# Epsilon added to the query features on VectorE, and output blocks evicted in 576 columns, in a fused convolution and linear-attention kernel

## The chip, the cores and the metric

The kernel runs on one core of a Trainium2 chip. The metric is the device time of one execution in microseconds; each version is run several times, and the median counts. A profiled execution gives a trace besides: which engine worked when, and on what. The engines are TensorE (PE in the profile, with its weight loads as PEld), VectorE (DVE), ScalarE (ACT), GpSimd (POOL) and SyncE (SP), which here only issues transfers (DMAs).

## The reference, cut to what matters

Two independent halves stand side by side in the last axis of the output, 576 columns each, for 2048 rows.

```python
# half A: a short convolution of k (4 taps), times v, then a causal convolution as long as the sequence, times q
for t in range(ks):
    k_shift = k_shift + k_pad[:, t:t + S, :] * shift_k[:, ks - 1 - t][None, None, :]
kv = k_shift * v
y_f = rfft(kv_pad) * rfft(kf_pad)          # length 2 * S
y = irfft(y_f)[:S] + kv * ssm_D
a = q * y
# half B: linear attention, 32 heads of 18 columns
phi = lambda t: jnp.where(t > 0, t + 1, jnp.exp(t)) + 1e-6
pq, pk = phi(q), phi(k)
kv = einsum("bhsd,bhse->bhde", pk, v);  z = einsum("bhsd->bhd", pk)
num = einsum("bhqd,bhde->bhqe", pq, kv)
den = einsum("bhqd,bhd->bhq", pq, z)[..., None] + 1e-6
b = (num / den) @ wo
```

Inputs and output are bfloat16. The change concerns the 1e-6 in `pq`, and the way in which the rows of `b` leave the chip.

## The kernel before, in words

**Half B.** x lies in four tiles of 512 rows; its transposes xT come from TensorE and PSUM for the first (L323) and by transposing transfers for the others (L347). Sixteen blocks of keys (L623) and twenty of queries (L644) are projected; ScalarE takes exp (L628, L647) and VectorE forms phi without the epsilon: pk by rows, and pqT, transposed, as two tiles of 128 x 5 x 1024 (feature in the partition, 126 features in each of four chunks and 72 in the fifth). G = x transposed times phi(k) (L673) is folded with the value weights into kv (L708), which is masked into heads as kvb (L711, L715), and with wo into M (L770), one 576 x 576 matrix in five chunks. The denominators (L744 to L761) become reciprocals, rden, which are written to DRAM and read back as rb, spread over the 18 features of each head; pqT is multiplied by rb in place, chunk by chunk, by VectorE or GpSimd (named pqn in the program). An output block of 128 rows is then five matmuls of pqT by M for each half of 288 columns (L813), each half evicted from its own PSUM bank into ob by ScalarE or VectorE, and one transfer of 144 KB for a block.

**The epsilon before.** (pq + 1e-6) times M is pq times M plus 1e-6 times the column sums of M over each head. The fifth chunk has only 72 features, so partitions 96 to 127 of it are free: there lie the 32 heads' reciprocals in pqT (two transfers from DRAM, named rh, after a memset at L280) and 1e-6 times the 32 column sums in M (ten matmuls, L798, an eviction by VectorE, L801, after a memset at L790). So the fifth chunk is contracted over 128 partitions.

**Half A.** The taps are VectorE products (L402) and sums, partly on GpSimd and partly by an accumulating transfer. The sequence is then transformed in two stages: 128-point matmuls by the table Gsb (L467, results Ch and Cu), VectorE transposes of 32x32 (L506), 16-point matmuls (L515, results sph and spu); a pointwise complex product of both (two products of 2048 columns, one of them with a copy X of sph whose neighbouring partitions are exchanged; 18 transfers on SP); the inverse 16-point stage (L551, results V) and 128-point stage (L576) by the table Esb; and the product with q. For two of three column groups an inverse result is evicted as yb first, and two such are multiplied at once.

**What sets the order.** Every step is recorded as an operation, and its engine and its place in the order come from a string, PLAN (a letter for the engine and the operation's number); PLACES gives each tile's address. Each engine runs its own list in that order and waits at the head of it. GpSimd's products wait for VectorE's last product ahead of them in the plan, so that the two take turns. SP issues nearly all transfers, in its order. Helpers record many operations under one line: L222 transfers, L229 ScalarE copies, L231 VectorE copies, L236 products and sums.

Of the kernel before, what the change touches and what calls it, by code (L numbers as in the profile page):

```python
# [13 lines left out]
S = 2048  # L14
D = 576
# [9 lines left out]
HDT = []  # L25
ACC = [(0, 1), (2, 1)]
# [88 lines left out]
def _tables():  # L115
# [11 lines left out]
    E = np.empty((128, 32 + 2, 128), np.float32)  # L127
# [3 lines left out]
    W = np.zeros((32, 3, 32), np.float32)  # L131
    for bb in range(16):
        for k1 in range(16):
            p = 2.0 * np.pi * ((k1 * bb) % 16) / 16.0
            c, s = np.cos(p), np.sin(p)
            W[bb, 0, 2 * k1] = c
            W[16 + bb, 0, 2 * k1] = s
            W[bb, 0, 2 * k1 + 1] = -s
            W[16 + bb, 0, 2 * k1 + 1] = c
            W[2 * k1, 1, 2 * bb] = c  # L140
# [8 lines left out]
    for i in range(2):  # L149
        E[:, 32 + i, :] = np.kron(np.eye(4), W[:, 1 + i, :])  # L150

# [17 lines left out]
    C[:, o:o + 8] = EPS  # L169
# [14 lines left out]
def kernel(  # L184
# [24 lines left out]
    w_d = nc.dram_tensor("w_scr", (4, D), BF, kind="Internal").ap()  # L209
# [24 lines left out]

    def tt(e, o, a, b, op):
        return (nc.vector if e == "DVE" else nc.gpsimd).tensor_tensor(out=o, in0=a, in1=b, op=op)  # L236
# [10 lines left out]
    Esb = SB("Esb", [128, 34, 128], side=1)  # L247
    srow = SB("srow", [64, D // 64, 4])
    srt = SB("srt", [64, 4, D // 64])
    wtok = P.buf("wtok", [128, 1], space="dram")  # L250
# [28 lines left out]
    for f in range(2):  # L279
        P.op("G", lambda e, f=f: nc.gpsimd.memset(pqT[f].t[64:128, 4, :], 0.0), wr=[(pqT[f], (4, g)) for g in (2 * f, 2 * f + 1)] + [(pqT[f], "r")], name="pqz", ms=1024, st="pqz%d" % f)  # L280
# [5 lines left out]
    load("srow", srow, lambda e: dma(e, srow.t[:], A_shift_k.rearrange("(p d) j -> p d j", p=64)), 4608, 72, engs=EARLY)  # L286
    for i in range(2):
# [3 lines left out]
    load("Esb", Esb, lambda e: dma(e, Esb.t[:].rearrange("p a c -> p (a c)"), E_d), 1114112, 8704)  # L291

    P.op("AD", lambda e: copy(e, srt.t[:], srow.t[:].rearrange("p d j -> p j d")), rd=[srow], wr=[srt], name="wjt", n=36)
    load("ww", None, lambda e: dma(e, ap(w_d, 0, [[D // 64, 64], [D, 4], [1, D // 64]]), srt.t[:]), 4608, 18, rd=[srt], wr=[wtok])
    load("wjb", Wj, lambda e: dma(e, Wj.t[:].rearrange("p j d -> p (j d)"), ap(w_d, 0, [[0, 128], [1, 4 * D]])), 589824, 4608,
         rd=[wtok], wr=[(Wj, 0), (Wj, 1)])
# [94 lines left out]
    def conv_piece(cc, bh):  # L391
# [12 lines left out]
        P.op("D", tap, rd=[kh, (Wj, 0)] + ([(Wj, 1)] if cc else []), wr=[(m, 0), (m, 2)], name="tap",  # L404
# [81 lines left out]
    def s2(C, cc, pp, nm):  # L486
# [23 lines left out]
        for kh in range(4):  # L510
            ps = psb(1, "s2ps")

            def mm(e, kh=kh, ps=ps):
                for j in range(4):
                    nc.tensor.matmul(  # L515
                        ps.t[32 * j:32 * j + 32, 0, :],
                        lhsT=W2()[32 * kh:32 * kh + 32, :], rhs=ct.t[32 * kh:32 * kh + 32, 8 * j:8 * j + 8],
                        start=True, stop=True)
            P.op("P", mm, rd=[ct, idw], wr=[ps], name="s2" + nm, st=st, mm=[(512, 32, 32)] * 4)
            P.op("AD", lambda e, kh=kh, ps=ps: copy(  # L520
                e, view(sp.t[:], 32 * kh, [[256, 8], [128, 2], [1, 32]]), ps.t[:, 0, :].rearrange("p (w k t) -> p w t k", w=8, t=2)),
                 rd=[ps], wr=[(sp, kh)], name="s2ev" + nm, n=512, st=st)
# [9 lines left out]
    def inv(g, su):  # L532
# [5 lines left out]
        xb = SB("X", [128, 16, 128])  # L538
        for i in range(2):
            load("X", xb, lambda e, i=i: dma(e, xb.t[i:128:2], tx.t[1 - i:128:2]), 262144, 4096, rd=[tx], wr=[(xb, i)])  # L540
        P.op("DG", lambda e: tt(e, xb.t[:], su.t[:], xb.t[:], ALU.mult),
             rd=[su], wr=[xb], name="p2", n=2048, x2=1, two=1, st=st)
        P.op("DG", lambda e: tt(e, tx.t[:], su.t[:], tx.t[:], ALU.mult),
             rd=[su], wr=[tx], name="p1", n=2048, x2=1, two=1, st=st)
        for hh in range(4):
            ps = psb(1, "i1ps")

            def mm(e, hh=hh, ps=ps):
                for c in range(4):
                    for wi, src in ((0, tx), (1, xb)):  # L550
                        nc.tensor.matmul(ps.t[:, 0, 128 * c:128 * c + 128], lhsT=src.t[:, 4 * hh + c, :], rhs=Esb.t[:, 32 + wi, :],  # L551
                                         start=(wi == 0), stop=(wi == 1))
            P.op("P", mm, rd=[tx, xb, Esb], wr=[ps], name="i1", st=st, mm=[(128, 128, 128)] * 8)

            def ev(e, hh=hh, ps=ps):
                copy(e, view(V[gi].t[:], c0 + 4 * hh, [[n, 32], [CC // 4, 4], [1, 4]]),
                     ps.t.rearrange("p b c -> p (b c)").rearrange("p (c j r) -> p r j c", j=4, r=32))
            P.op("AD", ev, rd=[ps], wr=[(V[gi], (g, hh))], name="i1ev", n=512, st=st)
# [4 lines left out]
    def inv2(gi):  # L563
# [5 lines left out]
        for bg in range(16 // nb):  # L569
# [10 lines left out]
            if gi in YA:  # L580
# [23 lines left out]
            ns = max(nb, 4)  # L604
# [30 lines left out]
    def qproj(c, g):  # L635
        h0, hn = HCH[c]
        ps = psb(1, "qps")
        eb = SB("eq", [128, 512])
# [3 lines left out]
        def mm(e):  # L642
            for t in range(5):
                nc.tensor.matmul(ps.t[0:hn, 0, :], lhsT=wq.t[0:KT[t], t, h0:h0 + hn], rhs=xT.t[0:KT[t], t, :],  # L644
                                 start=(t == 0), stop=(t == 4))
        P.op("P", mm, rd=[xT, wq], wr=[ps], name="q", mm=[(512, 128, 126)] * 5, st=st)
        P.op("A", lambda e: nc.scalar.activation(  # L647
            out=eb.t[0:hn], in_=ps.t[0:hn, 0, :], func=ACTF.Exp, bias=neg1.t[0:hn, :]), rd=[ps, neg1], wr=[eb],
             name="qexp", n=512, st=st)
        P.op("D", lambda e: nc.vector.scalar_tensor_tensor(  # L650
            out=pqT[g // 2].t[0:hn, c, 512 * (g % 2):512 * (g % 2) + 512], in0=eb.t[0:hn],
            scalar=1.0, in1=ps.t[0:hn, 0, :], op0=ALU.min, op1=ALU.max), rd=[ps, eb], wr=[(pqT[g // 2], (c, g))], name="qphi",
             n=512, st=st)
# [3 lines left out]
    for g in range(4):  # L657
        for c in range(5):
            qproj(c, g)
# [116 lines left out]
    for f in range(2):  # L776
# [3 lines left out]
        for c, (h0, hn) in enumerate(HCH):  # L780
            rb = SB("rb", [128, 1024])
# [3 lines left out]
            P.op("DG", lambda e, c=c, hn=hn, rb=rb, f=f: tt(e, pqT[f].t[0:hn, c, :], pqT[f].t[0:hn, c, :],  # L785
                                                           rb.t[0:hn, :], ALU.mult),
                 rd=[rb], wr=[(pqT[f], (c, g)) for g in (2 * f, 2 * f + 1)], name="pqn", n=1024, x2=1, two=1)
        load("rh", None, lambda e, f=f: dma(e, pqT[f].t[96:128, 4, :], ap(r_d, 1024 * f, [[2 * S, 32], [1, 1024]])), 65536, 2048,
             rd=[(rtok, (f, 0))], wr=[(pqT[f], "r")])
    P.op("G", lambda e: nc.gpsimd.memset(M.t[64:128, 4, :], 0.0), wr=[(M, 4), (M, "s")], name="Mz", ms=576)  # L790
    for c in range(5):
        b_M(c)
    sps = psb(2, "sps")

    def smm(e):
        for hh in range(2):
            for c, (h0, hn) in enumerate(HCH):
                nc.tensor.matmul(sps.t[:, hh, 0:HALF], lhsT=hmask()[0:hn, c, :],  # L798
                                 rhs=M.t[0:hn, c, HALF * hh:HALF * hh + HALF], start=(c == 0), stop=(c == 4))
    P.op("P", smm, rd=[(M, c) for c in range(5)] + [cst], wr=[sps], name="msf", mm=[(288, 126, 128)] * 10)  # L800
    P.op("D", lambda e: nc.vector.tensor_scalar(  # L801
        out=M.t[96:128, 4, :].rearrange("p (h c) -> p h c", h=2), in0=sps.t[96:128, :, 0:HALF], scalar1=EPS, scalar2=None,
        op0=ALU.mult), rd=[sps], wr=[(M, "s")], name="msev", n=576)

    def b_out(r):
        ob = SB("ob", [128, D])
        for hh in range(2):
            ps = psb(1, "ops")

            def mm(e, hh=hh, ps=ps):  # L810
                for c, (h0, hn) in enumerate(HCH):
                    kn = 128 if c == 4 else hn
                    nc.tensor.matmul(ps.t[:, 0, 0:HALF], lhsT=cols(pqT[r // 8].t[0:kn, c, 512 * (r // 4 % 2):512 * (r // 4 % 2) + 512], r),  # L813
                                     rhs=M.t[0:kn, c, HALF * hh:HALF * hh + HALF], start=(c == 0), stop=(c == 4))
            P.op("P", mm, rd=[(pqT[r // 8], (c, r // 4)) for c in range(5)] + [(pqT[r // 8], "r"), M], wr=[ps], name="out", mm=[(288, 126, 128)] * 5,
                 st="o%d" % (r // 2))
            P.op("AD", lambda e, hh=hh, ps=ps: copy(e, ob.t[:, HALF * hh:HALF * hh + HALF], ps.t[:, 0, 0:HALF]), rd=[ps],
                 wr=[(ob, hh)], name="oev", n=288, st="o%d" % (r // 2))
# [30 lines left out]
    with tc.manual_schedule():  # L849
        cnt, last = 0, None  # L850
        for o in order:
# [103 lines left out]
```

## Time and profile before

| what | value |
|---|---|
| device time, median of 3 runs | 160.0 us (159.97, 160.0, 162.04) |
| span of the profiled execution | 158.3 us |
| mean granted TensorE clock | 0.994 |
| transferred | 34.37 MB, mean 217 GB/s |

The span runs from the first to the last instruction in the trace; the device time of a run is about 1.7 us more. The profile's groups give busy time, the mean of one instruction in ns, and the idle time ahead of it with what ended it. Matmuls overlap in the pipeline, so the 286 ns of one are more than what a further one adds: ten projections of 288 columns add 1.23 us to the chain.

### The profile page before, as it was taken

What the parts mean: (1) busy time and instruction counts of PE and PEld (TensorE: products, weight loads), DVE (VectorE), ACT (ScalarE), POOL (GpSimd) and SP (SyncE); (2) the same over time, 40 slices, a digit from 0 to 9 for tenths busy, and PEclk for the clock granted to TensorE, in tenths of its full rate; (3) what the DMA queues carried; (4) which work ended last, traced back from release to release, by engine and by line L of the source; (5) the groups of instructions that cost most, each with busy time, mean ns of one, the idle gap of its engine ahead of it and who ended that gap; (6) DMA issues with size and microseconds to landing.
All of it is one profiled execution on the core that took longest, in us unless ns stands there. A gap on an engine that the chain in (4) does not pass through costs nothing.

```text
span 158.3 us, 4158 instructions
## 1 busy us (share of the span) xinstructions
PE 149.8 (95%) x1663; PEld 118.6 (75%) x1663; DVE 141.8 (90%) x170; ACT 125.1 (79%) x229; POOL 59.6 (38%) x53
## 2 busy tenths in 40 slices
PE   6899999999999999999999999999999999999960
PEld 2478885535679888788888887877767799999960
DVE  1547999999999998999999999999989999999690
ACT  4038999999996566467559699999899999998760
POOL 8801310011163554603611999799290000001520
PEclk9999999999999999999999999999999999999997
DMA  5999939999999809965546867881463599405766
GB/s 146 283 384 313 245 79 299 284 187 239 352 384 259 299 15 333 377 270 103 99 131 214 159 149 209 312 288 63 178 232 112 173 331 361 143 4 147 188 181 160
DMA packets 26317, 34.37 MB, mean 217 GB/s; under 512 B 15802, under 2 KB 20923, under 8 KB 25530
## 3 DMA queue, kind: packets, MB, share of 16 engines
q1 hardware_dynamic: 25754, 32.54, 66.6%
q0 software_dynamic: 544, 1.57, 5.6%
q8 instruction: 13, 0.21, 0.7%
q14 instruction: 6, 0.05, 0.1%
HBM read 20.86 MB, written 4.99 MB: 163 GB/s over the span
## 4 chain that ended last, share of the span: by engine, by line
PE 78%; ACT 8%; DVE 6%; DMA 2%; issue 1%; SPq 1%; DVEq 0%; ACTq 0%
PE ps_all L813 13%; PE ps_all L623 12%; PE ps_all L673 12%; PE ps_all L644 11%; PE ps_all L467 8%; PE ps_all L551 8%; PE ps_all L515 5%; ACT sph L229 3%; PE ps_all L576 3%; ACT V L229 3%; DMA x_sb<-in_B_x_dram 2%; PE ps_all L436 2%; DVE Ch L231 2%; ACT yb L229 1%; PE ps_all L708 1%
## 5 line engine op out<-in xcount | busy, mean ns | idle before, releaser
L644 PE MATMUL ps_all<-xT,wq 128*126 128x512 bf16 (+1 forms) x100 | 23.8, 381 | 0.1
L813 PE MATMUL ps_all<-M,pqT 126*128 126x288 bf16 (+1 forms) x160 | 22.5, 287 | 0.0
L623 PE MATMUL ps_all<-wk,xT 128*128 128x288 bf16 x160 | 20.4, 286 | 0.4 <-DVE xT L231 0.4
L402 DVE TENSOR_TENSOR m<-kh,Wj 128x6144 bf16<-128x6144 bf16 x6 | 20.1, 3349 | 0.0
L229 ACT ACTIVATE Cu<-ps_all 128x768 bf16<-128x768 f32 x22 | 17.3, 856 | 3.2 <-PE ps_all L467 3.2
L623 PEld LDWEIGHTS <-xT 128*128 128x128 bf16 x160 | 17.4, 110 | 3.1 <-DVE xT L231 0.6
L236 POOL TENSOR_TENSOR pqT<-pqT,rb 126x1024 bf16<-126x1024 bf16 (+1 forms) x9 | 19.1, 2174 | 1.0 <-DVE v L236 1.0
L813 PEld LDWEIGHTS <-pqT 126*128 126x128 bf16 (+1 forms) x160 | 16.6, 110 | 3.7 <-issue 1.9
L644 PEld LDWEIGHTS <-wq 128*126 128x126 bf16 (+1 forms) x100 | 12.5, 131 | 8.7 <-issue 2.2
L229 ACT ACTIVATE V<-ps_all 128x512 bf16<-128x512 f32 x32 | 17.2, 624 | 1.8 <-PE ps_all L551 1.8
L628 ACT ACTIVATE ek<-ps_all,neg 128x576 bf16<-128x576 f32 x16 | 11.9, 743 | 8.3 <-PE ps_all L623 8.3
L467 PEld LDWEIGHTS <-Gsb 128*128 128x128 bf16 x192 | 16.1, 98 | 2.6 <-issue 1.6
L551 PE MATMUL ps_all<-Esb,sph 128*128 128x128 bf16 x144 | 17.9, 219 | 0.1
L551 PE MATMUL ps_all<-Esb,X 128*128 128x128 bf16 x144 | 17.9, 219 | 0.0
L236 POOL TENSOR_TENSOR m<-m 128x1536 bf16<-128x1536 bf16 x4 | 12.4, 3096 | 13.1 <-DVE m L236 8.9
L673 PE MATMUL ps_all<-pk,x_sb 128*128 128x289 bf16 (+1 forms) x128 | 17.1, 287 | 0.0
L229 ACT ACTIVATE sph<-ps_all 128x512 bf16<-128x512 f32 x30 | 16.6, 608 | 0.2
L229 ACT ACTIVATE Ch<-ps_all 128x768 bf16<-128x768 f32 x19 | 15.2, 853 | 1.0 <-PE ps_all L467 0.8
L229 ACT ACTIVATE spu<-ps_all 128x512 bf16<-128x512 f32 x28 | 15.1, 613 | 0.6 <-PE ps_all L515 0.6
L236 POOL TENSOR_TENSOR q<-yb,q 128x384 bf16<-128x384 bf16 x4 | 3.6, 912 | 29.4 <-DVE yb L231 27.6
L673 PEld LDWEIGHTS <-x_sb 128*128 128x128 bf16 x128 | 12.3, 98 | 2.9
L551 PEld LDWEIGHTS <-sph 128*128 128x128 bf16 x144 | 14.0, 98 | 0.5 <-DVE sph L236 0.2
(96 smaller groups left out, 301.9 us busy)
## 6 DMA issues: line engine op xcount, KB each, us to landing
X<-sph SPq DMA_DIRECT2D x18, 256.0 KB
v<-in_A_v_dram SPq DMA_DIRECT2D x2, 1152.0 KB
out_dram<-ob SPq DMA_DIRECT2D x16, 144.0 KB
q<-in_A_q_dram SPq DMA_DIRECT2D x1, 2304.0 KB
out_dram<-q SPq DMA_DIRECT2D x12, 192.0 KB
rb<-r_scr SPq DMA_DIRECT2D x8, 252.0 KB
x_sb<-in_B_x_dram SPq DMA_DIRECT2D x3, 576.0 KB
kh<-in_A_k_dram SPq DMA_DIRECT2D x1, 1584.0 KB
```

The costliest lines, as they stand in the source:

```text
L229: nc.scalar.activation(out=o, in_=i, func=ACTF.Copy)
L236: return (nc.vector if e == "DVE" else nc.gpsimd).tensor_tensor(out=o, in0=a, in1=b, op=op)
L402: return nc.vector.tensor_tensor(out=m.t[:], in0=i0, in1=i1, op=ALU.mult)
L467: nc.tensor.matmul(ps.t[:, bank, lo - 384 * bank:hi - 384 * bank], lhsT=Gsb.t[:, b, ri, :], rhs=src[:, lo - CC * j:hi - CC * j], start=Tru ...
L515: nc.tensor.matmul(ps.t[32 * j:32 * j + 32, 0, :], lhsT=W2()[32 * kh:32 * kh + 32, :], rhs=ct.t[32 * kh:32 * kh + 32, 8 * j:8 * j + 8], st ...
L551: nc.tensor.matmul(ps.t[:, 0, 128 * c:128 * c + 128], lhsT=src.t[:, 4 * hh + c, :], rhs=Esb.t[:, 32 + wi, :], start=(wi == 0), stop=(wi == 1))
L576: nc.tensor.matmul(ps.t[:, 0, n * j:n * j + n], lhsT=Esb.t[:, 2 * b + ri, :], rhs=V[gi].t[:, 2 * b + ri, :], start=(ri == 0), stop=(ri == 1))
L623: nc.tensor.matmul(ps.t[:, hh, 0:HALF], lhsT=cols(xT.t[0:KT[t], t, :], r), rhs=wk.t[0:KT[t], t, HALF * hh:HALF * hh + HALF], start=(t == 0 ...
L628: P.op("A", lambda e: nc.scalar.activation(out=eb.t[:], in_=ps.t[:, :, 0:HALF], func=ACTF.Exp, bias=neg1.t[:]), rd=[ps, neg1], wr=[eb], na ...
L644: nc.tensor.matmul(ps.t[0:hn, 0, :], lhsT=wq.t[0:KT[t], t, h0:h0 + hn], rhs=xT.t[0:KT[t], t, :], start=(t == 0), stop=(t == 4))
L673: nc.tensor.matmul(ps.t[0:m, 0, 0:n], lhsT=x4[r // 4].t[:, r % 4, :] if t == 4 else x_sb[r // 4].t[:, r % 4, 128 * t:128 * t + 128], rhs=p ...
L813: nc.tensor.matmul(ps.t[:, 0, 0:HALF], lhsT=cols(pqT[r // 8].t[0:kn, c, 512 * (r // 4 % 2):512 * (r // 4 % 2) + 512], r), rhs=M.t[0:kn, c, ...
```

## The change

1. **Epsilon.** VectorE adds 1e-6 to each chunk of pqT in place, ahead of its product with rb: ten instructions, eight of 126x1024 and two of 72x1024 (named pqe, L837 of the changed kernel). The memsets at L280 and L790, the ten matmuls of L798, the eviction at L801 and the two transfers rh go; the fifth chunk is contracted over its 72 partitions.
2. **Output.** The ten matmuls of an output block are one operation on two PSUM banks, and one instruction evicts 576 columns: 16 evictions (15 on ScalarE, 1 on VectorE) in place of 32 of 288 columns (22 and 10).
3. **Second column group.** The last two results of its inverse stage are multiplied by q straight from PSUM, and go out in two transfers of 96 KB in place of one of 192 KB.
4. **Order.** PLAN and PLACES are new throughout. The transfers of X all come after M in SP's order; one GpSimd sum of 1536 columns fewer, one product of pqT more on GpSimd, three yb evictions fewer on VectorE.
5. Esb has 35 blocks in place of 34, the last unused; Wj is tracked in three pieces. Other branches that the diff brings (WX, ZP, ZA, MS2, MI1, MQ) are switched off and leave nothing in the program.

```diff
+MS2, MI1, MO, MQ = False, False, True, False
+EP, WX = True, False
...
-    for f in range(2):
-        P.op("G", lambda e, f=f: nc.gpsimd.memset(pqT[f].t[64:128, 4, :], 0.0), wr=[(pqT[f], (4, g)) for g in (2 * f, 2 * f + 1)] + [(pqT[f], "r")], name="pqz", ms=1024, st="pqz%d" % f)
+    if not EP:
+        for f in range(2):
...
-            if gi in YA:
+            ya = gi in YA and not (gi == 1 and bg >= 6)
+            if ya:
...
         for c, (h0, hn) in enumerate(HCH):
+            if EP:
+                P.op("D", lambda e, c=c, hn=hn, f=f: nc.vector.tensor_scalar(
+                    out=pqT[f].t[0:hn, c, :], in0=pqT[f].t[0:hn, c, :], scalar1=EPS, scalar2=None, op0=ALU.add),
+                     wr=[(pqT[f], (c, g)) for g in (2 * f, 2 * f + 1)], name="pqe", n=1024, two=1)
             rb = SB("rb", [128, 1024])
...
-        load("rh", None, lambda e, f=f: dma(e, pqT[f].t[96:128, 4, :], ap(r_d, 1024 * f, [[2 * S, 32], [1, 1024]])), 65536, 2048,
-             rd=[(rtok, (f, 0))], wr=[(pqT[f], "r")])
-    P.op("G", lambda e: nc.gpsimd.memset(M.t[64:128, 4, :], 0.0), wr=[(M, 4), (M, "s")], name="Mz", ms=576)
+        if not EP:
+            load("rh", None, lambda e, f=f: dma(e, pqT[f].t[96:128, 4, :], ap(r_d, 1024 * f, [[2 * S, 32], [1, 1024]])), 65536, 2048,
+                 rd=[(rtok, (f, 0))], wr=[(pqT[f], "r")])
...
     def b_out(r):
         ob = SB("ob", [128, D])
-        for hh in range(2):
-            ps = psb(1, "ops")
+        m = 2 if MO else 1
+        for h in range(0, 2, m):
+            ps = psb(m, "ops")
...
-                    kn = 128 if c == 4 else hn
-                    nc.tensor.matmul(ps.t[:, 0, 0:HALF], lhsT=cols(pqT[r // 8].t[0:kn, c, 512 * (r // 4 % 2):512 * (r // 4 % 2) + 512], r),
-                                     rhs=M.t[0:kn, c, HALF * hh:HALF * hh + HALF], start=(c == 0), stop=(c == 4))
+                        nc.tensor.matmul(ps.t[:, hh - h, 0:HALF], lhsT=cols(pqT[r // 8].t[0:128 if c == 4 and not EP else hn, c, 512 * (r // 4 % 2):512 * (r // 4 % 2) + 512], r),
+                                         rhs=M.t[0:128 if c == 4 and not EP else hn, c, HALF * hh:HALF * hh + HALF], start=(c == 0), stop=(c == 4))
...
-            P.op("AD", lambda e, hh=hh, ps=ps: copy(e, ob.t[:, HALF * hh:HALF * hh + HALF], ps.t[:, 0, 0:HALF]), rd=[ps],
-                 wr=[(ob, hh)], name="oev", n=288, st="o%d" % (r // 2))
+            P.op("AD", lambda e, h=h, ps=ps: copy(e, ob.t[:, HALF * h:HALF * (h + m)].rearrange("p (m c) -> p m c", m=m), ps.t[:, :, 0:HALF]), rd=[ps],
+                 wr=[(ob, h)], name="oev", n=288 * m, st="o%d" % (r // 2))
...
```

More of the change, by code (lines that the diff above doesn't have):

```diff
@@ L148, in _tables @@
     W[np.abs(W) < 1e-7] = 0.0
-    for i in range(2):
-        E[:, 32 + i, :] = np.kron(np.eye(4), W[:, 1 + i, :])
+    for i, wi in enumerate([3] if NW == 1 else [3, 1, 2]):
+        E[:, 32 + i, :] = np.kron(np.eye(4), W[:, wi, :])
     C1 = np.zeros((128, 128 + 32 + 128), np.float32)
@@ L233, in copy, with scale @@
             nc.gpsimd.tensor_copy(out=o, in_=i)
+    def scale(e, o, a, c):
+        if e == "ACT":
+            nc.scalar.activation(out=o, in_=a, func=ACTF.Copy, scale=c)
+        else:
+            nc.vector.tensor_scalar(out=o, in0=a, scalar1=c, scalar2=None, op0=ALU.mult)
     def tt(e, o, a, b, op):
@@ L246 @@
     Gsb = SB("Gsb", [128, 16, 2, 128], side=1)
[L247 to L250, printed above, removed]
+    Esb = SB("Esb", [128, 32 + NW, 128], side=1)
+    if ZP or ZA:
+        sgn = SB("sgn", [128, 2], FP32, side=1)
+    if WX:
+        Wr = SB("Wr", [128, D, 4])
+    else:
+        srow = SB("srow", [64, D // 64, 4])
+        srt = SB("srt", [64, 4, D // 64])
+        wtok = P.buf("wtok", [128, 1], space="dram")
+        w_d = nc.dram_tensor("w_scr", (4, D), BF, kind="Internal").ap()
     Wj = SB("Wj", [128, 4, D], side=1)
@@ L509, in s2, with mm @@
             rd=[C], wr=[ct], name="tr" + nm, n=nw * 32, tr=1, st=st)
-        for kh in range(4):
-            ps = psb(1, "s2ps")
-            def mm(e, kh=kh, ps=ps):
+        m = 2 if MS2 else 1
+        for k0 in range(0, 4, m):
+            ps = psb(m, "s2ps")
+            def mm(e, k0=k0, ps=ps):
                 for j in range(4):
[L515 to L522, printed above, removed]
+                    for kh in range(k0, k0 + m):
+                        nc.tensor.matmul(
+                            ps.t[32 * j:32 * j + 32, kh - k0, :],
+                            lhsT=W2()[32 * kh:32 * kh + 32, :], rhs=ct.t[32 * kh:32 * kh + 32, 8 * j:8 * j + 8],
+                            start=True, stop=True)
+            P.op("P", mm, rd=[ct, idw], wr=[ps], name="s2" + nm, st=st, mm=[(512, 32, 32)] * (4 * m))
+            P.op("AD", lambda e, k0=k0, ps=ps: copy(
+                e, view(sp.t[:], 32 * k0, [[32, m], [256, 8], [128, 2], [1, 32]]), ps.t.rearrange("p m (w k t) -> p m w t k", w=8, t=2)),
+                 rd=[ps], wr=[(sp, k) for k in range(k0, k0 + m)], name="s2ev" + nm, n=512 * m, st=st)
         if nm == "h":
@@ new lines, in inv @@
+        if z:
+            load("X", tx, lambda e: dma(e, tx.t[1:128:2], tx.t[0:128:2]), 262144, 4096, wr=[tx])
+        xs = su
+        if z and not za:
+            xs = SB("xs", [128, 16, 128])
+            for i in range(2):
+                load("xs", xs, lambda e, i=i: dma(e, xs.t[i:128:2], su.t[1 - i:128:2]), 262144, 4096, rd=[su], wr=[(xs, i)])
+        if z:
+            P.op("DA", lambda e: scale(e, xb.t[:], xb.t[:], sgn.t[:, int(za):int(za) + 1]), rd=[sgn], wr=[xb], name="sgn", n=2048, two=1, st=st)
@@ L543, in inv @@
+        P.op("DG", lambda e: tt(e, xb.t[:], xs.t[:], xb.t[:], ALU.mult),
+             rd=[xs], wr=[xb], name="p2", n=2048, x2=1, two=1, st=st)
         P.op("DG", lambda e: tt(e, tx.t[:], su.t[:], tx.t[:], ALU.mult),
              rd=[su], wr=[tx], name="p1", n=2048, x2=1, two=1, st=st)
[L545 to L556, printed above, removed]
+        if za:
+            for i in range(2):
+                load("zacc", tx, lambda e, i=i: nc.gpsimd.dma_start(out=tx.t[i:128:2], in_=xb.t[1 - i:128:2], accum_op=ALU.add),
+                     262144, 4096, rd=[xb], wr=[(tx, 2 * i), (tx, 2 * i + 1)], engs="G")
+        elif z:
+            P.op("DG", lambda e: tt(e, tx.t[:], tx.t[:], xb.t[:], ALU.add),
+                 rd=[xb], wr=[tx], name="zadd", n=2048, x2=1, two=1, st=st)
@@ new lines, in inv, with mm, ev @@
+        m = 2 if MI1 else 1
+        for h0 in range(0, 4, m):
+            ps = psb(m, "i1ps")
+            def mm(e, h0=h0, ps=ps):
+                for hh in range(m):
+                    for c in range(4):
+                        for wi, src in ((0, tx),) if z else ((1, tx), (2, xb)):
+                            nc.tensor.matmul(ps.t[:, hh, 128 * c:128 * c + 128], lhsT=src.t[:, 4 * (h0 + hh) + c, :], rhs=Esb.t[:, 32 + wi, :],
+                                             start=(wi < 2), stop=(wi != 1))
+            P.op("P", mm, rd=[tx, Esb] + ([] if z else [xb]), wr=[ps], name="i1", st=st, mm=[(128, 128, 128)] * ((4 if z else 8) * m))
+            def ev(e, h0=h0, ps=ps):
+                copy(e, view(V[gi].t[:], c0 + 4 * h0, [[n, 32], [CC // 4, 4], [1, 4 * m]]),
@@ L657 @@
     for g in range(4):
-        for c in range(5):
-            qproj(c, g)
+        for c, m in ((0, 2), (2, 2), (4, 1)) if MQ else [(c, 1) for c in range(5)]:
+            qproj(c, m, g)
     GT = SB("GT", [128, 5, D])
@@ L795, in smm @@
-    def smm(e):
-        for hh in range(2):
[L797 to L803, printed above, removed]
+    if not EP:
+        sps = psb(2, "sps")
+        def smm(e):
+            for hh in range(2):
+                for c, (h0, hn) in enumerate(HCH):
+                    nc.tensor.matmul(sps.t[:, hh, 0:HALF], lhsT=hmask()[0:hn, c, :],
+                                     rhs=M.t[0:hn, c, HALF * hh:HALF * hh + HALF], start=(c == 0), stop=(c == 4))
+        P.op("P", smm, rd=[(M, c) for c in range(5)] + [cst], wr=[sps], name="msf", mm=[(288, 126, 128)] * 10)
+        P.op("D", lambda e: nc.vector.tensor_scalar(
+            out=M.t[96:128, 4, :].rearrange("p (h c) -> p h c", h=2), in0=sps.t[96:128, :, 0:HALF], scalar1=EPS, scalar2=None,
+            op0=ALU.mult), rd=[sps], wr=[(M, "s")], name="msev", n=576)
@@ L863 @@
                     last = ins
-                elif last is not None:
+                elif o.eng == "POOL" and last is not None:
                     tc.add_manual_dep(ins, last.name, mybir.DependencyInfo(mybir.DependencyClass.Sync, mybir.DependencyReason.SCHED_ONLY),
```

160 lines of the change are left out of this document (88 added, 72 removed), and 31 rows, old and new, of the table PLACES.

## Prediction, made before the changed kernel was run

> **What bounds the kernel now.** I read the engine shares on the page first, then the stretches, then the chain that ended last, and last the groups of instructions that the change touches.
>
> ```profile
> span 158.3 us, 4158 instructions
> PE 149.8 (95%) x1663; PEld 118.6 (75%) x1663; DVE 141.8 (90%) x170; ACT 125.1 (79%) x229; POOL 59.6 (38%) x53
> ...
> DMA  5999939999999809965546867881463599405766
> GB/s 146 283 384 313 245 79 299 284 187 239 352 384 259 299 15 333 377 270 103 99 131 214 159 149 209 312 288 63 178 232 112 173 331 361 143 4 147 188 181 160
> ...
> PE 78%; ACT 8%; DVE 6%; DMA 2%; issue 1%; SPq 1%; DVEq 0%; ACTq 0%
> ```
>
> TensorE works in 95% of the span and holds 78% of the chain; VectorE stands close behind at 90%. An average over stages tells no limit, so the stretches come next (busy us of PE, PEld, DVE, ACT, POOL, then granted clock, DMA share, GB/s).
>
> ```profile
> 12.00:39.00 27.00, 26.50 (x288) 17.68 (x287) 26.07 (x32) 26.05 (x44) 4.00 (x9) 1.00 1.01 236
> 39.00:95.00 56.00, 56.00 (x524) 46.00 (x523) 55.28 (x57) 40.64 (x66) 25.82 (x14) 1.00 0.74 224
> 95.00:99.00 4.00, 3.73 (x50) 2.82 (x47) 3.87 (x7) 4.00 (x8) 4.00 (x2) 1.00 0.72 210
> 99.00:124.00 25.00, 25.00 (x331) 18.56 (x326) 23.68 (x33) 23.91 (x52) 15.58 (x7) 1.00 0.54 193
> 124.00:140.00 16.00, 15.92 (x250) 15.01 (x242) 16.00 (x17) 15.40 (x34) 0.00 (x0) 1.00 0.66 241
> 140.00:158.00 18.00, 13.09 (x187) 12.77 (x184) 12.55 (x23) 11.40 (x25) 3.56 (x4) 0.96 0.56 149
> ```
>
> From 39 to 95 us TensorE is full and VectorE has 56.00 − 55.28 = 0.72 us to spare; from 124 to 140 VectorE is full. So TensorE carries the time, and VectorE is a second bound with hardly any reserve: what the change takes from TensorE counts only as far as VectorE follows. The chain shows the places outside TensorE (start, length, what).
>
> ```profile
> 5.43 1.38 DVE x L231
> ...
> 8.20 3.85 PE ps_all L623 x30
> ...
> 33.85 2.56 ACT sph L229 x5
> ...
> 93.92 1.39 PE ps_all L708 x25
> ...
> 99.58 1.30 PE ps_all L798 x10
> ...
> 133.77 1.81 ACT V L229 x4
> ...
> 154.13 0.47 DVEq L950
> ```
>
> They are the start (the first projection begins at 8.20), ScalarE's evictions near 34 and 134 us, and the end. For the end, the timeline shows TensorE's last stretch and VectorE's last:
>
> ```profile
> 149.96 3.13 PE L576 MATMUL ps_all<-V,Esb 128*128 128x192 bf16 x36
> 153.57 1.03 DVE L236 TENSOR_TENSOR q<-yb,q 128x768 bf16<-128x768 bf16 x2
> ```
>
> TensorE ends at 149.96 + 3.13 = 153.09; eviction, product, issue and the last output transfer take 158.3 − 153.1 = 5.2 us more. VectorE's last product ends at 154.60, so issue and transfer are 3.7 of them. The device time has a median of 160.0 us over three runs (159.97, 160.0, 162.04), 1.7 above this span; I sum on the span and add 1.7.
>
> **The change, part by part.** The groups that it touches (busy us, mean ns of one):
>
> ```profile
> L236 DVE TENSOR_TENSOR pqT<-pqT,rb 126x1024 bf16<-126x1024 bf16 x1 | 0.7, 684 | 0.0
> L236 POOL TENSOR_TENSOR pqT<-pqT,rb 126x1024 bf16<-126x1024 bf16 x7 | 15.0, 2172 | 1.0 <-DVE v L236 1.0
> L280 POOL MEMSET pqT<- 64x1024 bf16 x2 | 1.9, 947 | 0.1
> L790 POOL MEMSET M<- 64x576 bf16 x1 | 0.6, 578 | 0.1
> L801 DVE TENSOR_SCALAR M<-ps_all 32x576 bf16<-32x576 f32 x1 | 0.8, 767 | 0.0
> L231 DVE CAST M<-ps_all 126x576 bf16<-126x576 f32 x3 | 2.3, 758 | 0.1
> L229 ACT ACTIVATE M<-ps_all 126x576 bf16<-126x576 f32 x1 | 0.7, 651 | 0.0
> L229 ACT ACTIVATE ob<-ps_all 128x288 bf16<-128x288 f32 x22 | 8.6, 442 | 0.5 <-issue 0.3
> L231 DVE CAST ob<-ps_all 128x288 bf16<-128x288 f32 x10 | 4.5, 447 | 1.3 <-PE ps_all L813 1.1
> L231 DVE CAST yb<-ps_all 128x384 bf16<-128x384 f32 x6 | 3.3, 553 | 0.3 <-ACT yb L229 0.2
> L231 DVE CAST V<-ps_all 128x512 bf16<-128x512 f32 x4 | 2.7, 683 | 0.1
> L813 PE MATMUL ps_all<-M,pqT 126*128 126x288 bf16 x128 | 20.5, 286 | 0.0
> L813 PE MATMUL ps_all<-M,pqT 128*128 128x288 bf16 x32 | 9.2, 288 | 0.0
> L755 DVE TENSOR_SCALAR den<-ps_all,dcol 128x256 f32<-128x256 f32 x2 | 0.9, 436 | 0.0
> L236 DVE TENSOR_TENSOR hT<-hT,Drow 1x64 bf16<-1x64 bf16 x1 | 0.2, 170 | 0.0
> L231 DVE COPY x<-x_sb 128x128 bf16<-128x128 bf16 x1 | 1.4, 1371 | 4.0 <-DMA x_sb<-in_B_x_dram 4.0
> ```
>
> *The contraction rows.* The ten matmuls of L798 go: 1.30 us in the chain, between other TensorE work that stays, so −1.30. L801 (0.77 us, VectorE), the two memsets of pqT (1.9 us, GpSimd, before any reader exists), that of M and two 64 KB transfers into pqT go too; GpSimd is 38% busy and these stand behind other work, so I count nothing for them. Contracting 72 instead of 128 rows in every fifth output matmul saves no time: 128 rows take 288 ns, 126 take 286.
>
> *The ten steps on pqT.* Ten VectorE additions of a constant (L837 of the changed kernel), eight on 126x1024, two on 72x1024, in place. The trace has no such instruction. The lower bound is a VectorE row of next to no elements, 170 ns, so 1.7 us for ten; the upper is one element at a time, as in the PSUM reads: from 436 ns for 256 columns to 758 for 576 is 1.01 ns a column, so 1.2 us for 1024 and 12.1 for ten. The nearest row is the product on the very same tile, 684 ns, so I take 0.684 each, 6.8 us, as an upper value of that choice, since a step with a constant reads one operand less. [...]
>
> *What else VectorE gains and loses.* Output evictions: ten of 288 go (−4.47) and one of 576 comes (+0.76). By the two instruction orders set side by side, VectorE has three yb evictions fewer (−1.66), L801 (−0.77) and the one pqT product (−0.68) gone to nothing or GpSimd, two V evictions more (+1.37), and smaller moves, by their rows, that come to −0.97; in all −6.4. With 6.8 for the new steps the total is +0.4: no relief. Eight of the ten steps stand ahead of kvb (L715), the step behind the 1.39 us of L708 on which M and every output wait. VectorE's rows up to there add up to 85.0 us before and 86.1 after. Of these 1.1 us it can take 0.72 out of its reserve between 39 and 95, so at most +0.4 us is left; with 0.684 as an upper value I take half, +0.2. Behind a late step queue VectorE's transposes, and behind these TensorE's second stage.
>
> *Output in 576 columns.* ScalarE: 22 of 288 columns (9.7 us) become 15 of 576 (15 x 651 ns = 9.8), and its other moves cancel within half a microsecond. So nothing is won there; the ten that VectorE is rid of pay for the new steps. A block now needs two PSUM banks at once, and ten matmuls before it can be evicted.
>
> *GpSimd's queue.* It takes over one product of pqT (+2.17): five for the second half of the rows behind the eighth step, 10.9 us, and four behind the tenth, 8.7 us. By the VectorE rows the first outputs of the second half come some 13 us after that eighth step, those of the first half some 12 after the tenth: covered by 2 to 4 us. If that cover is gone, the outputs start late by what is missing.
>
> *The start and SP's queue.* The first copy of x, 1.38 us on VectorE with 128x128 in 1371 ns, goes to another engine, but the k weights land at about the same time, so I take −0.1. The small weight copy comes earlier, and with it the transposing loads behind it on SP; ScalarE stays full there (26.05 of 27), so nothing counted.
>
> *The end.* The last TensorE work becomes an output block instead of an inverse stage, evicted in 0.65 us and sent: 0.65 + 3.7 + 0.05 = 4.4 us instead of 5.2, so −0.8.
>
> Sum: 158.3 − 1.3 + 0.2 − 0.1 − 0.8 = 156.3; ScalarE's stalls and all other waits are taken as they are. With 1.7 around it, 158.0.
>
> **The rivals.** *Faster: the stalls go too.* The chain shows the pace of each kind of block where nothing holds it up, for instance:
>
> ```profile
> 21.47 1.08 PE ps_all L644 x5
> ...
> 27.11 1.23 PE ps_all L623 x10
> ```
>
> All blocks at such a pace come to 147.1 us (an estimate from the chain's pieces). That leaves 6.0 us of TensorE's 153.1 without work: some 2.2 at the start, 2.2 from 12 to 39, 1.4 after 95. A whole new order can take the last two; for it speaks that the ten steps may cost little and that ScalarE has fifteen fixed costs fewer in its queue; against it, that ScalarE's sum is the same. With half, 156.2; with all of it, and the steps cheap enough to hide, 158.0 − 0.2 − 3.6 = 154.2.
>
> *Slower: the copied halves of sph come late.* The row of their issues (count, shortest, median and longest ns, first and last start):
>
> ```profile
> L222 SPq DMA_DIRECT2D X<-sph x18: 470/540/3473, 41.5 to 123.1; - x18
> ```
>
> Before, the 18 transfers of 256 KB begin at 41.5 us; in the new order all 18 follow M, with Esb, the rest of rb and the first outputs: 8.2 MB in about 27 us, 305 GB/s. The slices from 126 to 134 us reach 331 and 361, so it fits. Against that stands 236 GB/s in the stretch 12 to 39, where the DMA share is 1.01: then they take 34.7 us, and the products and L551 behind them wait up to 7.7, so 165.7. It decides below 8.2 MB / (27 + 5.2) = 255 GB/s. For it speaks the density; against it, that the new order leaves about 35 steps between the last of them and their product.
>
> *Slower: the steps run at one element at a time.* At 1.2 instead of 0.684 us they put 8 x 0.52 = 4.2 us more ahead of kvb, and nothing of it in reserve: 158.0 + 0.2 + 4.2 = 162.4; it decides above 1.3.
>
> *Slower: GpSimd shuts VectorE out.* The row for it is the copy of 128x128 in 1371 ns, during GpSimd's first memsets, where ScalarE needs about 0.3. The eighth step and GpSimd's product are put one after the other by the order itself, but the last two steps can meet a product of 2.17 us: about +2, 160.0. [...]
>
> *Nothing measurable:* what TensorE loses VectorE takes, 159 to 160.
>
> **How the numbers follow.** My forecast (157 to 159) has 0.36; the stalls gone too 0.29; nothing 0.12; GpSimd in the way 0.09; late X 0.09; slow steps 0.05. The predicted time is 158.0. Below 154.2 every gain would have to come true together; above 163.2 only late X goes by its price. The range 154.8 to 163.0 leaves out the full recovery of stalls and the worst of late X. Two per cent, about what a measurement of this kernel can tell from no change, is 3.2 us: below 156.8 lie the recovered stalls and a little of the forecast, 0.31; above 163.2 late X, half of the slow steps and a rest for mishaps in the new order, 0.16; between them 0.53.
>
> **What would show it.** Right: no L798 group, the new steps at 0.3 to 0.7 us, sixteen output evictions of about 0.65, kvb within 1 us of 95.4, the end 4.4 us behind TensorE's last. Wrong: steps above 1.2 us or in the shadow of GpSimd; idle time of VectorE or TensorE released by the DMA of X; kvb 3 us late; TensorE waiting for pqT from GpSimd; or ScalarE's waits near 34 and 134 us gone.

## The result, and the profile after

The changed kernel takes 165.2 us (median of four runs, 164.6 to 166.0) where the kernel before takes 160.0: the ratio is 1.031, with a 95% interval of 1.024 to 1.038. It is slower; 158.0 was forecast, and 163.0 was the upper end of the range. Ratios leave disturbed runs out and medians do not, so below the ratio counts where the two differ (most in e13, where three of six runs were disturbed).

The profiled execution has a span of 163.0 us (device time 164.8). The page's head, shares of busy time and slices:

```profile
span 163.0 us, 4116 instructions
PE 151.7 (93%) x1653; PEld 117.9 (72%) x1653; DVE 140.8 (86%) x166; ACT 126.6 (78%) x224; POOL 57.1 (35%) x52
...
PE   6599999999999989999999997999999999999970
...
PEclk9999999999999999999999998589999999999998
...
PE 64%; DMA 11%; DVE 9%; ACT 5%; SPq 5%; issue 1%; POOL 1%; ACTq 0%; DVEq 0%
```

VectorE and GpSimd are busy for less time than before, TensorE and ScalarE for 1.9 and 1.5 us more; TensorE has ten matmuls fewer, and part of them runs at half clock, as shown below. TensorE's share of the chain is 64% in place of 78, and transfers and SP's queue, 3% before, hold 16%. The row PEclk has a dip that was not there. The stretches say where the 4.7 us of span come in (columns as before: length, busy us of PE, PEld, DVE, ACT, POOL, clock, DMA share, GB/s):

```profile
39.00:95.00 56.00, 55.05 (x489) 44.49 (x488) 55.64 (x60) 38.92 (x66) 25.21 (x16) 1.00 0.56 172
95.00:99.00 4.00, 3.67 (x49) 2.89 (x48) 3.84 (x6) 4.00 (x6) 4.00 (x3) 1.00 0.73 178
99.00:124.00 25.00, 23.42 (x265) 15.60 (x266) 21.03 (x29) 20.92 (x38) 16.06 (x7) 0.86 0.73 245
```

In the 25 us from 99 on, TensorE gets 265 matmul records done in place of 331, at a mean clock of 0.86, and VectorE and ScalarE stand idle for 4 us each (1.3 and 1.1 before). That is the main place. In this trace some 1.3 us are lost earlier: kvb comes at 96.73, in the kernel before at 95.39.

```profile
96.73 0.23 DVE L770 TENSOR_TENSOR kvb<-ps_all,cst 72x72 bf16<-72x72 f32 x1 [0.16 <-PE ps_all L763]
```

The groups of the change itself behave:

```profile
L837 DVE TENSOR_SCALAR pqT<-pqT 126x1024 bf16<-126x1024 bf16 x8 | 3.2, 413 | 0.0
L240 ACT ACTIVATE ob<-ps_all 128x576 bf16<-128x576 f32 x15 | 9.7, 657 | 3.2 <-issue 2.0 <-DVE q L253 0.7 <-PE ps_all L874 0.2
L253 POOL TENSOR_TENSOR pqT<-pqT,rb 126x1024 bf16<-126x1024 bf16 x8 | 17.0, 2224 | 8.0 <-DMA rb<-r_scr 5.8 <-DVE pqT L837 2.2
```

The steps last 0.41 us, the evictions 0.66. But GpSimd waits 5.8 us for a transfer of rb. SP's timeline around it, with what it issued and when:

```profile
80.08 1.20 SPq L233 DMA_DIRECT2D r_scr<-rden  x2
81.33 0.50 SPq L233 DMA_DIRECT2D wv<-in_B_wqkv_dram  x1
83.45 2.54 SPq L233 DMA_DIRECT2D rb<-r_scr  x3
86.10 0.50 SPq L233 DMA_DIRECT2D wo<-in_B_wo_dram  x1
86.65 0.81 SPq L233 DMA_DIRECT2D rb<-r_scr  x1
87.50 0.54 SPq L233 DMA_DIRECT2D wv<-in_B_wqkv_dram  x1
88.09 0.57 SPq L233 DMA_DIRECT2D r_scr<-rden  x1
88.76 0.80 SPq L233 DMA_DIRECT2D rb<-r_scr  x1
89.61 0.56 SPq L233 DMA_DIRECT2D r_scr<-rden  x1
90.21 0.73 SPq L233 DMA_DIRECT2D wo<-in_B_wo_dram  x1
93.01 0.54 SPq L233 DMA_DIRECT2D X<-sph  x1
99.71 0.83 SPq L233 DMA_DIRECT2D rb<-r_scr  x1
```

Read it from the bottom. From 93.5 to 99.7 SP issues nothing; its list of waits says for what (total, times, longest):

```profile
SPq L233 <- DMA r_scr<-rden: 7.7, 2, 6.1
```

It waits for the second half of its own writes of rden, for the first half of the rows. These values were ready on VectorE at 78.28 + 3.35 = 81.6:

```profile
78.28 3.35 DVE L816 RECIPROCAL rden<-den 128x256 bf16<-128x256 f32 x2
```

In the kernel before, SP issues these writes at 80.24, ahead of every rb load, and wo already at 40.8 and 58.9:

```profile
80.24 1.09 SPq L222 DMA_DIRECT2D r_scr<-rden  x2
81.56 13.04 SPq L222 DMA_DIRECT2D rb<-r_scr  x7
```

In SP's new order the writes stand behind four rb loads, wo and a piece of wv, 1.6 MB together, so they are issued at 88.1 and 89.6. GpSimd's accumulating transfer of 768 KB is issued between them, at 88.8, and the DMA engines are 87% busy from 86 to 93 us. In the chain the first writes of rden take 2.6 us to land and the 81 KB that close wo 9.7, and TensorE's wait for them is one entry of its list:

```profile
80.76 2.63 DMA r_scr<-rden
...
90.21 9.71 DMA wo<-in_B_wo_dram
...
99.96 1.21 PE ps_all L825 x6
```

```profile
PE ps_all L825 <- DMA wo<-in_B_wo_dram: 1.1, 1, 1.1
```

Behind this gap the granted clock is 0.50 from 100.4 to 107.2 us:

```profile
101.00:102.00 1.00, 1.00 (x9) 0.50 0.57 201
102.00:104.00 2.00, 2.00 (x21) 0.50 0.87 285
104.00:106.00 2.00, 2.00 (x11) 0.50 0.91 229
106.00:107.00 1.00, 1.00 (x7) 0.50 0.90 204
```

So the profile offers several culprits at one place, and it can't tell which of them sets the time.

### The profile page after: what moved, and what is told of

Read it like the earlier page. It is cut to its first block, busy times and chain, and to the rows that moved or that the text cites. A ratio compares the mean times of both kernels' runs of the same rounds, so it can differ in the third digit from the quotient of the medians.

```text
span 163.0 us, 4116 instructions
## 1 busy us (share of the span) xinstructions
PE 151.7 (93%) x1653; PEld 117.9 (72%) x1653; DVE 140.8 (86%) x166; ACT 126.6 (78%) x224; POOL 57.1 (35%) x52
## 4 chain that ended last, share of the span: by engine, by line
PE 64%; DMA 11%; DVE 9%; ACT 5%; SPq 5%; issue 1%; POOL 1%; ACTq 0%; DVEq 0%
PE ps_all L699 13%; PE ps_all L874 11%; PE ps_all L604 10%; PE ps_all L677 9%; PE ps_all L728 6%; DMA wo<-in_B_wo_dram 6%; SPq L233 5%; PE ps_all L549 5%; PE ps_all L499 4%; PE ps_all L629 4%; DMA wk<-in_B_wqkv_dram 3%; DVE pk L685 3%; ACT spu L240 2%; DMA r_scr<-rden 2%; PE ps_all L468 2%
## 5 line engine op out<-in xcount | busy, mean ns | idle before, releaser
L253 POOL TENSOR_TENSOR pqT<-pqT,rb 126x1024 bf16<-126x1024 bf16 (+1 forms) x10 | 21.2, 2227 | 8.0 <-DMA rb<-r_scr 5.8
L874 PE MATMUL ps_all<-M,pqT 126*128 126x288 bf16 (+1 forms) x160 | 23.2, 296 | 0.6 <-ACT ob L240 0.2
L874 PEld LDWEIGHTS <-pqT 126*128 126x128 bf16 (+1 forms) x160 | 17.4, 112 | 4.4 <-issue 1.6
L240 ACT ACTIVATE Ch<-ps_all 128x768 bf16<-128x768 f32 x20 | 15.8, 859 | 5.9 <-PE ps_all L499 5.8
L240 ACT ACTIVATE V<-ps_all 128x512 bf16<-128x512 f32 x30 | 16.7, 628 | 1.3 <-PE ps_all L604 1.0
L702 ACT ACTIVATE eq<-ps_all,neg 126x512 bf16<-126x512 f32 (+1 forms) x20 | 13.5, 715 | 4.7 <-PE ps_all L699 2.5
L240 ACT ACTIVATE Cu<-ps_all 128x768 bf16<-128x768 f32 x21 | 16.3, 860 | 0.7 <-PE ps_all L499 0.6
L685 DVE SCALAR_TENSOR_TENSOR pk<-ek,ps_all 128x576 bf16<-128x576 bf16 x16 | 11.7, 747 | 4.1 <-ACT ek L682 4.0
```

The lines of the kernel that those rows point to most:

```text
L240: nc.scalar.activation(out=o, in_=i, func=ACTF.Copy)
L685: P.op("D", lambda e: nc.vector.scalar_tensor_tensor(out=pk[r // 4].t[:, r % 4, 0:D].rearrange("p (h c) -> p h c", h=2), in0=eb.t[:], scal ...
L702: P.op("A", lambda e: nc.scalar.activation(out=eb.t[0:hn], in_=ps.t[0:hn], func=ACTF.Exp, bias=neg1.t[0:hn, :]), rd=[ps, neg1], wr=[eb], n ...
L874: nc.tensor.matmul(ps.t[:, hh - h, 0:HALF], lhsT=cols(pqT[r // 8].t[0:128 if c == 4 and not EP else hn, c, 512 * (r // 4 % 2):512 * (r // ...
```

## The experiments

Four theories. **1:** the late end of wo makes a gap of 1.08 us, and the half clock behind it costs 3.4 us (6.8 us at half speed). **2:** the ten VectorE steps cost the time. **3:** the 18 transfers of X, all behind wo in SP's order, crowd the queues. **4:** SP stands for the late writes of rden, and everything behind them in its queue is late. Edits are to the changed kernel where nothing else is said; in PLAN, S stands for an issue on SP, D and A for VectorE and ScalarE, and the diffs show only the tokens that matter ("..." for the rest).

**e1, the end of wo early.**

```diff
-... S261 S223 ... A501 ... S224 ...
+... S261 S223 S224 ...
```

> The changed kernel with one transfer moved: the last 72 rows of wo (81 KB) are issued by SP straight behind the rest of wo, ahead of two rb loads, a tail of wv and two writes of rden. Theory 1 (that transfer lands late; TensorE stands still for 1.08 us behind it, and its granted clock then is 0.5 for 6.8 us, which costs 3.4 us): no gap before the fifth chunk of M, the clock stays at 1.00, and the time falls by about 4.5 us to 160.7. Theory 2 (the ten VectorE steps cost the time) and theory 3 (18 transfers of X crowded behind M): at most the 1.1 us of the gap go, 164 or more.

Measured: 165.8 us, ratio 1.040 (1.033 to 1.047) to the kernel before. The gap and the half clock are gone (mean clock 1.00), and nothing is won. Theory 1 falls as the cause of the time. TensorE's holes open later, from 110 to 120 us:

```profile
110.00:120.00 10.00, 6.24 (x103) 4.22 (x103) 6.40 (x10) 7.14 (x15) 9.35 (x5) 1.00 0.84 309
```

The chain shows what is late next: an output transfer, 144 KB behind transfers of X, whose buffer ScalarE wants again.

```profile
108.27 8.74 DMA out_dram<-ob
117.01 0.02 issue
117.03 0.04 ACTq L240
117.07 0.04 issue
117.11 0.66 ACT ob L240
```

**e2, the gap filled.**

```diff
         def mm(e):
+            if c == 4:
+                for j in range(12):
+                    nc.tensor.matmul(ps.t[:, 0, 0:256], lhsT=Gsb.t[:, 0, 0, :], rhs=Gsb.t[:, 1].rearrange("p a c -> p (a c)"),
+                                     start=True, stop=True)
```

> The changed kernel with twelve extra matmuls (128x256, results never read) ahead of the fifth chunk of M, so that TensorE works while it waits for the late rows of wo, which stay as late. Theory 1: the clock stays at 1.00, the time falls by about 3.4 us to 162, though the transfer lands no earlier. If the lateness itself and not the clock costs the time: 165 or a little more.

Measured: 164.1 us, ratio 1.027 (1.020 to 1.033); from 95 to 140 us the clock stays at 1.00. Without the filling it was 0.50 from 100.4 to 107.2 us, so the half clock went with that gap. The time is 1.1 us less at the median, with overlapping intervals, so a gain is not shown; 3.4 us less would be a ratio of 1.011, which lies outside the interval.

**e3, no steps.**

```diff
+            if o.name == "pqe":
+                continue
             ins = o.fn(o.eng)
```

> The changed kernel without the ten VectorE steps; it leaves the epsilon of the query features out. Theory 2: up to 4 us less, 161. Theory 1: the wait for wo and the clock stay, so 164 to 165.2.

Measured: 164.8 us, ratio 1.028 (1.025 to 1.031): 4 us of VectorE work less, and no difference that this comparison shows. Theory 2 falls for this order.

**e4 and e7, the epsilon part alone, in the order of the kernel before.** e7 takes the contraction rows out and puts nothing in their place; e4 has the ten steps as well.

```diff
-                    kn = 128 if c == 4 else hn
+                    kn = hn
...
+            if o.name in ("pqz", "Mz", "msf", "msev", "rh"):
+                continue
             ins = o.fn(o.eng)
...
-D84 A214 ... D87 P277
+D84 D837 D838 D839 D840 D841 A214 ... D87 D832 D833 D834 D835 D836 P277
```

> The kernel before, in its own order, with the epsilon part alone: the ten matmuls, their eviction, the memsets and the two transfers out, ten VectorE steps in (five ahead of kvb, five behind M), output still in 288 columns. Theory 1 (the new order is at fault, not the epsilon): 158.5 to 160, between the 1.3 us of the ten matmuls and nothing. Theory 2: 162 or more.

> The kernel before without its contraction rows (matmuls, eviction, memsets and the two transfers) and without steps in their place; it leaves the epsilon of the query features out. TensorE-bound reading: 158.7 (160.0 less 1.3). With e4 it gives the price of the ten steps in that order: 3.7 us if so, about what they last on VectorE.

Measured: e4 162.4 us, ratio 1.015 (1.012 to 1.018); e7 160.1 us, ratio 1.000 (0.998 to 1.003). So the ten matmuls, 1.30 us in the chain of before, were worth nothing (at most 0.3 us by the interval), and the steps cost 1.4% in that order, 2.3 us. In e7 the chain has another piece at the place of the ten matmuls: TensorE waits for VectorE.

```profile
101.11 0.87 DVE v L236
101.98 0.05 issue
102.03 0.83 PE ps_all L467 x8
```

The kernel before has the same product at the same place: GpSimd waits for it there, to 100.97, and the ten matmuls end at 100.88.

```profile
100.97 10.53 POOL L236 TENSOR_TENSOR pqT<-pqT,rb 126x1024 bf16<-126x1024 bf16 x5 [1.00 <-DVE v L236]
```

So the matmuls had filled a time in which TensorE would have waited for that product. The trace of e7 runs 1.1 us late from its start on; counted from kvb (95.39 before, 96.47 in e7), the product ends after 5.5 us in both.

**e5 and e6, the writes of rden early.** Both writes of the first half go behind those of the second (and in e6 the end of wo too, as in e1).

```diff
-... S255 S256 S221 D234 ... S264 ... D260 S239 ... S238 ...
+... S255 S256 S221 D234 S239 S238 ... S264 ... D260 ...
```

> The changed kernel with SP's two writes of rden for the first half of the rows issued right behind those of the second half (near 82 us in place of 88 and 90), ahead of the rb loads, wo and the tail of wv. Theory 4 (SP stands 6 to 7 us, to about 100 us, for these writes, which lie in full DMA queues, and the rest of rb, all X but one, Esb and the first outputs queue behind it): SP goes on near 94 us, X and rb land up to 6 us earlier, TensorE's holes between 100 and 120 us close in part: 161 to 162. If the lateness of that queue is covered: 165.

> The same with the last rows of wo early as well (as in e1). Theory 4 together with theory 1: neither hole nor slow clock is left, 160 to 161. If the ten steps or the transfers of X as such hold the kernel up: 163 or more.

Measured: e5 161.2 us, ratio 1.005 (1.003 to 1.008); e6 161.4, ratio 1.007 (1.005 to 1.009). Two tokens on SP bring back some 2.5 of the 3.1%, and the end of wo adds nothing to that. In e5 SP waits 0.4 us in all for writes of rden, in place of 7.7, and in the stretch from 99 us the three engines are nearly full:

```profile
SPq L233 <- DMA r_scr<-rden: 0.4, 1, 0.4
```

```profile
99.00:124.00 25.00, 24.37 (x327) 17.56 (x327) 24.80 (x32) 24.32 (x45) 15.46 (x7) 1.00 0.85 297
```

TensorE's records are 327 in place of 265, at full clock, though all 18 transfers of X still stand behind wo in SP's order (the first starts at 92.35, before M is done), at 297 GB/s. So theory 4 holds, and theory 3 falls as a cause by itself: the transfers of X fit, if they start on time. GpSimd's wait for rb falls from 5.8 to 3.0 us. Which of the late transfers (rb, X or output) cost most is not separated.

**e8 and e14, no steps with the transfers on time.** e8 is e6 without the ten steps, e14 is e9 (below) without them, by the edit of e3.

> e6 without the ten VectorE steps; it leaves the epsilon of the query features out. If VectorE is a second bound once the transfers are on time, the steps cost 2 to 4 us here (against 0.4 in e3, where the late transfers covered them): 157 to 159. If not, no more than 0.5 below e6.

> e9 without the ten VectorE steps; it leaves the epsilon of the query features out. If the steps are covered in the new order once its transfers are on time: 159.8, as e9. If VectorE is the bound there: 156.5 to 158.

Measured: e8 161.6 us, ratio 1.007 (1.004 to 1.010), e6's own; e14 160.6 us, ratio 0.999 (0.996 to 1.002), no lower than e9. In the new order the steps are covered, late transfers or not; in the old one (e4) they are not.

**e9, the copy of x.** A candidate for what is left between e5 and the kernel before stands in the chain at 58 us: a copy on VectorE that lasts four and a half times as long as one on ScalarE (rows of the changed kernel).

```profile
L242 DVE COPY x<-x_sb 128x256 bf16<-128x256 bf16 x1 | 1.8, 1832 | 0.0
L240 ACT ACTIVATE x<-x_sb 128x256 bf16<-128x256 bf16 x1 | 0.4, 407 | 0.0
```

The timeline of the changed kernel shows what runs beside it: GpSimd's product from 56.87 to 59.98, the copy from 58.24 to 60.07.

```profile
56.87 3.11 POOL L253 TENSOR_TENSOR v<-m,v 128x1536 bf16<-128x1536 bf16 x1 [3.54 <-DVE m L434]
58.24 1.83 DVE L242 COPY x<-x_sb 128x256 bf16<-128x256 bf16 x1
```

```diff
-... D47 ...
+... A47 ...
```

> The kernel of e5 with one copy of 128x256 (the last 64 columns of a tile of x) on ScalarE in place of VectorE. In e5 it lasts 1.74 us on VectorE, in the chain, and ends when GpSimd's product of 3.1 us beside it ends; on ScalarE the same shape takes 0.43. If that blocking is what is left between e5 and the kernel before: about 1.2 us less, 160.0. If VectorE's other work takes the place: 161.

Measured: 159.8 us, ratio 0.996 (0.994 to 0.998), 0.9% below e5. This version beats both kernels, by 0.4% against the one before, and kvb comes at 95.34. That the copy is slow because of the product beside it is argued: in e5 too it ends 0.09 us behind the product (59.41 and 59.32), but no run has this copy on VectorE clear of one.

**e10 and e12, output in halves.** e10 is e5, e12 is e9, each with two evictions of 288 columns for a block.

```diff
-copy(e, ob.t[:, HALF * h:HALF * (h + m)].rearrange("p (m c) -> p m c", m=m), ps.t[:, :, 0:HALF])
+[copy(e, ob.t[:, HALF * i:HALF * (i + 1)], ps.t[:, i, 0:HALF]) for i in range(2)][-1]
```

> The kernel of e5 with each output block evicted by two instructions of 288 columns in place of one of 576. ScalarE gets 15 x (2 x 0.442 - 0.657) = 3.4 us more. If the 576 columns are worth something on the path: 162 to 163; if ScalarE's share there is covered: 161.2.

> e9 and e10 together: the writes of rden early, the copy of x on ScalarE, each output block evicted in two halves of 288 columns. e9 gave 159.8 against 160.1 of the kernel before, e10 160.6 against 161.2 of e5. If the halves cost nothing or gain: 159.2 to 159.8. If the 576 columns are worth their 3.4 us of ScalarE once the copy is off the path: above 160.5.

Measured: e10 160.6 us, ratio 1.002 (0.998 to 1.005); e12 160.1 us, ratio 0.995 (0.992 to 0.999). Neither is slower than its pair with 576 columns: what ScalarE saves there is not on the path.

**e11 and e13, the lateness put into the kernel before.** e11 issues the two writes behind the five rb loads of the second half; e13 also puts wo behind four of these loads. X stays as early as before.

```diff
-... S225 ... S226 ... S253 ... S254 ... S241 ... S240 ... S263 ... S255 ... S259 ... S261 ... S257 ... S246 ...
+... S253 ... S254 ... S263 ... S255 ... S259 ... S261 S225 S226 ... S257 S241 S240 ... S246 ...
```

> The kernel before, in its own order but for SP's two writes of rden for the first half of the rows, which are issued behind the five rb loads of the second half, as in the changed kernel. Theory 4 by the order of these writes alone: rb of the first half some 5 us later, 161 to 163. If the lateness costs only together with the 18 transfers of X behind it: 160.

> The kernel before, in its own order but for SP's: wo whole is issued behind four rb loads (in the changed kernel behind three) and the two writes of rden for the first half behind the fifth, as good as in the changed kernel; the transfers of X that were early stay early. Theory 4 (the late writes cost because wo fills the queues ahead of them, and M waits for wo): 162 to 165. If it takes the 18 transfers of X behind them too: 160 to 161.

(The diff is e13's; e11 leaves S225 and S226, wo, where they were.) Measured: e11 160.3 us, ratio 1.000 (0.997 to 1.002); e13 163.8 us, ratio 1.015 (1.010 to 1.019). The writes alone are covered in the old order, in which SP waits 2.7 us for them at the longest. With wo loaded into the same microseconds the kernel before slows by 1.5%, but not by a longer stand of SP: its waits for writes of rden are 4.2 us in all and 2.7 at the longest, against 4.1 and 2.7 in e11. The accumulating transfer of the taps takes 10.2 us in place of 6.4, and GpSimd's sum behind it starts 2.20 us late:

```profile
96.59 3.09 POOL L236 TENSOR_TENSOR m<-m 128x1536 bf16<-128x1536 bf16 x1 [2.20 <-DMA m<-m]
99.65 2.12 POOL L236 TENSOR_TENSOR pqT<-pqT,rb 126x1024 bf16<-126x1024 bf16 x1
99.72 2.87 DVE L236 TENSOR_TENSOR v<-m,v 128x1536 bf16<-128x1536 bf16 x1
```

VectorE's product of that sum now runs beside a product on GpSimd and lasts 2.87 us, where it took 0.95 in the kernel before, clear of that product. TensorE waits for it:

```profile
PE ps_all L467 <- DVE v L236: 1.7, 1, 1.7
```

So e13 does not carry the changed kernel's fault over into the old order. It shows that wo among the rb loads costs time there by another path, a late sum and a product that meets GpSimd's.

## Why the prediction was wrong, point by point

- *"so I take 0.684 each"*: 0.413 us measured. The product on the same tile, 684 ns, was far off as a stand-in for the step. It did not matter to the time: the steps are free in this order (e8, e14).
- *"The ten matmuls of L798 go ... so −1.30"*: wrong. e7 shows 0.0. They stood in the chain, but a product of VectorE came due where they ended. I asked what covers the removed work and not what comes due when it goes, though the windows said that VectorE had 0.72 us to spare in 56.
- *The failed step:* *"ScalarE's stalls and all other waits are taken as they are"*, and in it *"The start and SP's queue"*, which follows only the small weight copy and the transposing loads. That wo (from 41 and 59 us to 86 and 90) and two writes of rden (from 80 to 88) were moved in among the rb loads is in the order and was put at nothing. e5 gives the price of the writes: 2.5%, 4 us. Ahead of them stood rb, wo and wv, with an accumulating transfer beside them, and a write of 64 KB took 9.5 us, from 90.2 to 99.7, against 2.6 us for the first ones; SP stood still for 6.1 of them.
- *"Slower: the copied halves of sph come late"*: its 165.7 lies close to the measured 165.2 by chance. From 95 us on no engine's wait that the profile of the changed kernel lists ends at a transfer of X; the waits for transfers there are TensorE's for wo (1.1 us) and GpSimd's for rb (5.8). I asked whether the rate suffices (255 GB/s needed); it does (297 in e5). All of X but one did start late (100.7 us), but because SP stood still for six microseconds ahead of it.
- *"Slower: GpSimd shuts VectorE out"*: not at the steps, which last 0.41 us each, clear of GpSimd's products. A copy of x meets one, lasts 1.83 us and ends 0.09 us behind it; moving it to ScalarE is worth 0.9% (e9). That the product holds the copy up is argued and not shown. kvb, which I expected within 1 us of 95.4, comes at 96.73, and at 95.34 in e9.
- *"0.65 + 3.7 + 0.05 = 4.4"* behind TensorE's last work: 4.9. ScalarE evicts the last block only after eight inverse results and a wait of 0.7 us for VectorE's last product, at 158.36, 0.24 us behind TensorE's end. So the end gains 0.3 us, not 0.8. With the failed step and the copy put right, e9 still takes 159.8, 1.8 above the forecast; the ten matmuls (1.3) and the end (0.5) were overrated by as much.

What stays open: SP stood 2.7 us for the late writes in e11 and in e13, and e11 lost nothing; in the new order it stands 6.1 us, with the rest of rb, most of X and the outputs behind it. Which of these sets the time there, and what makes a write of 64 KB take 9.5 us, was not tried.

## What to carry to other kernels

When an order is written anew, walk down the queue that issues the transfers, not only the engines: for each write that a later load waits for, ask what now stands ahead of it, and what stands still behind it. A piece in the chain is worth its length only if nothing else comes due within that length; e7 is the cheapest test of that. And of several culprits at one place, the one that looks worst (here a gap and a half clock) may only be covering the next.

## What the runs showed of the hardware

- The timeline of the changed kernel, TensorE at its gap:

```profile
98.47 0.41 PE L549 MATMUL ps_all<-ct,idw 32*32 32x512 bf16 x8
99.96 1.21 PE L825 MATMUL ps_all<-wo,kvb 72*72 72x288 bf16 x6 [1.08 <-DMA wo<-in_B_wo_dram]
```

  A gap of 1.08 us, with only eight 32x32 matmuls in the half microsecond ahead of it, was followed by 6.8 us at a granted clock of 0.50, and by 3.4 us of it in e3, where the gap is 1.06 us; with the gap filled (e2) or gone (e1, e5) the clock stayed at 1.00 there. A longer gap left the clock up: in e1 TensorE stands still for 3.06 us, to 117.8, and the clock is 1.00 from 110 to 130 us. What makes the difference was not tried.
- Two small transfers landed late in the changed kernel: 81 KB of wo, issued at 90.2, took 9.7 us, and a write of 64 KB 9.5, with the DMA engines 87% busy from 86 to 93 us. The accumulating transfer, issued at 88.8 and 10.4 us on its way, that write (99.7) and the 81 KB (99.9) end within a microsecond; no run here shows what ties them.
